# A two-stage attention and SwiGLU kernel: weight loads split by matrix, and a new order of work at the start of the first tile

## The chip, the cores and the metric

The kernel runs on one core of one Trainium2 chip. The metric is the device time of one execution in microseconds (us). Before the change three runs gave a median of 244.1 us (243.9 to 244.66). One more execution was recorded by the hardware profiler, and all times inside the kernel are from that one, counted from the start of its span.

The engines are called as the profile calls them: PE is TensorE (matrix products), DVE VectorE, ACT ScalarE, POOL GpSimd, SP SyncE. They run their own instruction lists in order and wait for each other by semaphores. PSUM is the memory that PE writes; it has eight banks here, each 128 x 512 float32.

## What is computed

For 4 batches, 8 heads, 768 positions and a head size of 64, an attention with a narrow window, and a SwiGLU block on its result:

```python
scores = scale * np.matmul(q, k.transpose(0, 1, 3, 2))
keep = is_global | is_local          # 8 global keys, 96 local ones
scores = np.where(keep, scores + bias, -1e9)
a = softmax(scores)
x = np.matmul(a, v)                  # heads side by side: 3072 tokens x 512
g = x @ w_gate                       # 512 x 1536
silu = g * (1.0 / (1.0 + np.exp(-g)))
out = (silu * (x @ w_val)) @ w_out   # 1536 x 512
```

## The kernel before

All work is emitted by one Python function in an order written out by hand; each engine executes its own instructions in that order. Inputs are float32 in memory and are cast to float16 by the loading DMAs, which POOL issues (k, q, v, all weights). The loads of one queue go out one after another; each uses one of eight semaphores in turn, so a ninth load is issued only after the first has landed.

**Two stages in one stream.** Tokens are worked in eight tiles of 384 (`TB`): tile t is half of batch t // 2. Attention gives `xT`, four chunks of 128 x 384 for each tile (c = 0 to 3: two from each quad of heads). The FFN of a tile runs over f = 0 to 11, each f being 128 of the 1536 hidden columns: a *gate* (four matmuls, one for each c, into one PSUM bank), a *value* (four more into another bank), and later `out_part`s (three matmuls of 512 columns each) that multiply the hidden tile with `w_out`. Attention work of the next half is put between the f steps.

**Gate and value** (`products`, `gate_or_val`, lines 538 to 564). After a gate's four matmuls ACT makes `th` = tanh(g/2) from the bank (L558) and DVE makes `sl` = (th + 1) * g from `th` and the bank (L560). After the value DVE multiplies it with `sl` into `hT` (L564). A bank is free for the next user when its last reader is done: a gate's bank after `sl`, a value's after `hT`.

**Banks.** Four banks a0 to a3 are handed out in turn by `bank`, three banks x0 to x2 by `spare`, and o0 is used by name. The head of the run uses all of them by name for batch 0's first half.

**The start** (lines 602 to 682). POOL issues k and q of the first half of batch 0, v, then gate and value weights in columns of two f (`load_w(0, 2)`: four DMAs), k and q of the second half for heads 0 to 3, weights for f 2 and 3, k and q for heads 4 to 7, weights for f 4 to 7, the rest of v, weights for f 8 to 11, then w_out. Each `load_w` goes through 256 rows at a time (g = 0 holds chunks c 0 and 1, g = 1 chunks 2 and 3). Meanwhile the four head pairs of the first half are turned (`p_tr`: transposes on PE, copies by DVE and ACT) and scored (`p_bias`, `p_sc`: a matmul that writes the position bias, then the scores on top), ACT takes the exponentials (L361), PE the sums (`denominators`) and products with v (`numerators`), DVE scales these into `xT` (L497). The part of v that belongs to chunk 3 is a small tile of its own, `vCut`.

Then the first FFN tile begins. Its first gates and values (f 0 and 1, lines 677 to 682) are started chunk by chunk as the chunks of `xT` become ready: c 0 and 1 of both, then c 2, then c 3.

**The rest of tile 0** (lines 762 to 770 and 824 to 843). For each f: gate, value, and after some f a step of the second half of batch 0: `trh(h0, h1)` turns two pairs (24 transposes into o0 and one spare bank; for pairs 0 and 1 all eight copies run on ACT, L316 and L330, for pairs 2 and 3 most run on DVE), `sch(hp)` scores one pair (it takes a0 to a3: six bias matmuls L339, then ten score matmuls L350, then four exponentials on ACT), `va(0, g, 1)` makes a half of `xT`. The order is: f 0, f 1, trh(0, 1), f 2, sch(0), f 3, sch(1), trh(2, 3), f 4, f 5, sch(2), f 6, sch(3), f 7, va, f 8, va, f 9 to 11.

**Tile 1's first steps** (line 771). `n_out` says after which f an `out_part` of tile 0 is put: (1, 0) means after f 0 and f 2. The part after f 2 is the fourth of the first row block, which needs the last piece of w_out; after f 2 too, two pairs of batch 1 are turned.

Of the kernel before, what the change touches and what calls it, by code (L numbers as in the profile page):

```python
# [9 lines left out]
FP32 = mybir.dt.float32  # L10
# [27 lines left out]
def kernel(  # L38
# [12 lines left out]
    nc = tc.nc  # L51
# [10 lines left out]
    NC = DM // 128  # L62
    J = S // 128
    NCH = 7
    TB = 384
# [25 lines left out]
    sb2 = ctx.enter_context(tc.tile_pool(name="sb2", bufs=2))  # L91
# [25 lines left out]
    def load_half(half, h0, h1):  # L117
        for st, src in ((k16, k), (q16, q)):
            nc.gpsimd.dma_start(out=st[:, half, h0:h1], in_=half_of(src, half, h0, h1))  # L119
# [21 lines left out]
    def make_slope(eng, h):  # L141
        eng(slopeI[:, h, :], ident, -slopes[h] / scale)
# [63 lines left out]
    wg = sb.tile([128, NC, DFF], FP16, name="wg")  # L206
    wv = sb.tile([128, NC, DFF], FP16, name="wv")
    wo = sb.tile([128, NFF, DM], FP16, name="wo")
    def load_w(f0, f1):
        a, z = 128 * f0, 128 * f1  # L210
        for g in range(2):
            for w, src in ((wg, moe_w_gate), (wv, moe_w_val)):
                nc.gpsimd.dma_start(  # L213
                    out=w[:, 2 * g:2 * g + 2, a:z],
                    in_=src[256 * g:256 * g + 256, a:z].rearrange("(p s) f -> p s f", s=2))

    def load_wo(g):
        nc.gpsimd.dma_start(
            out=wo[:, 3 * g:3 * g + 3, :],
            in_=moe_w_out[384 * g:384 * g + 384].rearrange("(f p) d -> p f d", p=128))  # L220
# [4 lines left out]
    def x_of(t):  # L225
        if t not in xTs:
            xTs[t] = sb2.tile([128, NC, TB], FP16, name="xT", tag="xT", bufs=4)
        return xTs[t]
# [5 lines left out]
    def bank(name, dt=FP32):  # L234
        tag = state["tags"][state["n"] % len(state["tags"])]
        state["n"] += 1
        return single(name, tag, dt)

    def banks(name, dt=FP32):
        return [bank(name, dt) for _ in range(2)]  # L240

    def spare(name, dt=FP32):
        tag = state["x"][gv.get("n", 0) % len(state["x"])]
        gv["n"] = gv.get("n", 0) + 1
        return single(name, tag, dt)

    def single(name, tag, dt=FP32):
        return ps.tile([128, 512 if dt == FP32 else 1024], dt, name=name, tag=tag)
# [8 lines left out]
    def run_later(n):  # L257
        for _ in range(n):
            if later:
                later.pop(0)()  # L260
# [273 lines left out]
    hTs = {}  # L534

    gv = {}

    def products(t, f, which, c0, c1, dst=None):
        if f == 0 and which == 0 and c0 == 0:
            hTs[t] = sb2.tile([128, NFF, TB], FP16, name="hT", tag="hT", bufs=3)  # L540
        if c0 == 0:
            if dst is None:
                dst = spare("gv"[which] + "ps")
            gv[f, which] = dst
        w = (wg, wv)[which]
        for c in range(c0, c1):
            nc.tensor.matmul(  # L547
                gv[f, which][:, 0:TB], lhsT=w[:, c, 128 * f:128 * f + 128],
                rhs=x_of(t)[:, c, :],
                start=(c == 0), stop=(c == NC - 1))  # L550

    def gate_or_val(t, f, which, c0=0):
        products(t, f, which, c0, NC)
        dst = gv.pop((f, which))

        if which == 0:
            th = sb2.tile([128, TB], FP32, name="th", tag="th")
            nc.scalar.activation(out=th, in_=dst[:, 0:TB], func=AF.Tanh, scale=0.5)  # L558
            sl = sb2.tile([128, TB], FP32, name="sl", tag="sl")
            nc.vector.scalar_tensor_tensor(  # L560
                out=sl, in0=th, scalar=1.0, in1=dst[:, 0:TB], op0=AluOp.add, op1=AluOp.mult)
            gv["sl"] = sl
        else:
            nc.vector.tensor_mul(hTs[t][:, f, :], dst[:, 0:TB], gv["sl"])  # L564

    ops_t = {}

# [34 lines left out]
    for c in range(3):  # L602
        load_v_rest(0, c)
    nc.gpsimd.dma_start(
        out=vCut[NG:NG + cut], in_=v[0, :, 3 * KC:TB, :].rearrange("h p d -> p h d"))
# [9 lines left out]
    def p_bias(hp, which, *tags):  # L615
        pairs[0, hp].sc = pairs[0, hp].bias(0, which, [single("sc", t) for t in tags])

    def p_sc(hp, which, *tags):
        if tags:
            p_bias(hp, which, *tags)  # L620
        pairs[0, hp].scores_half(0, which, pairs[0, hp].sc)

    def p_tr(hp, kt, qt, q_eng):
        tr = [single("trs", t, FP16)[:, 0:TB] for t in (qt, kt)]
        pairs[0, hp].turn_half(0, tr)
        pairs[0, hp].copy_half(0, tr, V, q_eng)

    V, A = nc.vector.tensor_copy, nc.scalar.copy
# [8 lines left out]
    nc.sync.dma_start(out=vCut[0:NG], in_=vG[:, 0])  # L637
    for h in range(4, 8):
        make_slope(nc.vector.tensor_scalar_mul, h)
    load_w(0, 2)  # L640
    load_half(1, 0, 4)
    load_w(2, 4)
    load_half(1, 4, 8)
    load_w(4, 8)
    for c in range(3, NCH):
        load_v_rest(0, c)
    load_w(8, 12)
    load_wo(0)
    load_wo(1)
    load_wo(2)  # L650
# [5 lines left out]
    for c in range(NCH):  # L656
        load_v_rest(1, c)
    p_bias(0, 0, "a0", "a1")
    p_tr(1, "x2", "o0", V)
    p_sc(0, 0)  # L660
    p_sc(0, 1, "a2", "a3")
    p_sc(1, 0, "x0", "x1")
    p_tr(2, "a0", "a1", V)
    p_sc(1, 1, "x2", "o0")
# [9 lines left out]
    for side, tag in enumerate(("x0", "x1")):  # L674
        quads[0, 1].numerators(side, single("num", tag))

    head = [(0, 0), (0, 1), (1, 0), (1, 1)]
    hb = [banks("gvps"), banks("gvps")]
    for c0, c1, f0, f1 in ((0, 2, 0, 2), (2, 3, 0, 1), (3, 4, 0, 1), (2, 4, 1, 2)):
        for f, which in head:  # L680
            if f0 <= f < f1:
                products(0, f, which, c0, c1, hb[f][which])

    def sc(b, *units):
        def step():
# [14 lines left out]
    def va(b, g, half):  # L702
        return lambda: quads[b, g].values(half, bank, nc.vector)
# [7 lines left out]
    def trh(h0, h1, by_engine):  # L711
        def step():
            b0, b1 = single("trs", "o0", FP16), spare("trs", FP16)
            (a, b), (c, d) = [(t[:, 0:TB], t[:, TB:2 * TB]) for t in (b0, b1)]
            k_eng, last = (V, V) if by_engine else (A, A)
            pair_of = [(h0, (c, a)), (h1, (d, b))] if by_engine else [(h0, (b, a)), (h1, (d, c))]
            for hp, tr in pair_of:
                pairs[0, hp].turn_half(1, tr)
            for hp, tr in pair_of:
                pairs[0, hp].copy_half(1, tr, k_eng, A if hp == h0 else last)  # L720
        return step

    def sch(hp):
        def step():
            p = pairs[0, hp]
            scs = [p.bias(1, 0), p.bias(1, 1)]
            for which in range(2):
                p.scores_half(1, which, scs[which], which == 1 and hp != 1)
        return step
# [9 lines left out]
    def first(t, b):  # L739
        return {(t, 2): [tr(b, 0), tr(b, 1)],  # L740
                (t, 4): [sc(b, (0, 0), (0, 1), (1, 0))],
                (t, 5): [tr(b, 2), tr(b, 3)],
                (t, 6): [sc(b, (1, 1), (2, 0), (2, 1))],
                (t, 8): [sc(b, (3, 0), (3, 1))],
                (t, 9): [va(b, 0, 0)],
                (t, 10, 1): [va(b, 1, 0), lambda: run_later(len(later))]}
# [11 lines left out]
    def second(t, b):  # L758
        return {(t, 0): [sc(b, (0, 2), (1, 2))], (t, 3): [sc(b, (2, 2), (3, 2))],
                (t, 7): [vas(b, 1)]}  # L760

    half1 = {(0, 1): [trh(0, 1, False)], (0, 2): [sch(0)],
             (0, 3): [sch(1), trh(2, 3, True)], (0, 5): [sch(2)], (0, 6): [sch(3)],
             (0, 7): [va(0, 0, 1)], (0, 8): [va(0, 1, 1)]}

    def ff(t, f0, f1, n_out=(0,)):
        return [(t, f, n_out[(f - f0) % len(n_out)]) for f in range(f0, f1)]

    stretches = [
        (ff(0, 0, 10) + ff(0, 10, 12, (1,)), half1),  # L770
        (ff(1, 0, 4, (1, 0)) + ff(1, 4, 10, (1,)) + ff(1, 10, 12, (2,)), first(1, 1)),
        (ff(2, 0, 12, (1,)) + ff(3, 0, 12, (1,)), both(2, 1)),
        (ff(4, 0, 12, (1,)) + ff(5, 0, 12, (1,)), both(4, 2)),
        (ff(6, 0, 12, (1,)), second(6, 3)),
# [2 lines left out]
    loads, after = {}, {}  # L777
# [41 lines left out]
    def take(step_list):  # L819
        run_later(len(later))  # L820
        for step in step_list:
            step()

    for tiles, steps in stretches:
        for t, f, n_out in tiles:
            for ld in loads.pop((t, f), []):
                ld()
            if f == 0:
                while any(fn.__name__ in ("spread", "spread_first", "scale") for fn in later):
                    run_later(1)  # L830
            for which in range(2):
                run_later(1)
                gate_or_val(t, f, which, NC if t == 0 and f < 2 else 0)
                for fn in after.pop((t, f, which), []):
                    fn()
            for n in range(n_out):
                if (t, f, n) in steps:
                    take(steps.pop((t, f, n)))
                run_later(1)
                out_part(*outs.pop(0))  # L840
            if (t, f) in steps:
                take(steps.pop((t, f)))
        assert not steps
# [40 lines left out]
```

## Time and profile before

| | us |
|---|---|
| runs, median | 244.1 |
| runs, lowest and highest | 243.9, 244.66 |
| profiled execution, whole | 244.26 |
| its span, first to last instruction | 242.5 |
| PE busy | 235.2 (97% of the span) |
| DVE, ACT, POOL busy | 166.1, 129.2, 96.7 |
| PE idle, 15.60 to 28.18 | 12.58 - 11.27 = 1.31 |
| PE idle, 28.18 to 47.60 | 0.00 |
| PE idle, 47.60 to 60.00 | 0.52 |
| PE idle, 60 to 231 | 0.00 |

How to read it. PE's busy time is the union of its matmuls, and a matmul of 384 columns is shown with 0.33 us though the next one starts 0.16 us after it: they overlap. So a gate's four matmuls take 0.65 us of PE's time (the gates from 37.86 and 39.17 us have their values at 38.52 and 39.82), and a wait shorter than about 0.16 us beyond the usual step does not appear as idle time at all. What PE loses is best read from starts: when did this matmul start, and when would it have, had it followed the one before at the usual step? The granted TensorE clock is full in all 40 slices of the span. HBM reads and writes come to 144 GB/s over the span, but the first 50 us move near 200 GB/s of landed data, and there the DMAs are always busy.

### The profile page before, as it was taken

To read this page: it belongs to the slowest core of one execution; us is meant where nothing else is said; L and a number is where in the kernel's file an instruction comes from. 1 tells how busy PE (TensorE), PEld (TensorE's weight loads), DVE (VectorE), ACT (ScalarE), POOL (GpSimd) and SP (SyncE) were. 2 spreads that over 40 slices of the span, in tenths; PEclk is the share of its full clock that TensorE was granted. 3 is DMA by queue.
4 is the path that set the end of the run, shared out by engine and by line. 5 is a ranking of instruction groups with operands and counts; after the bars stand their busy time and mean duration, and the time that the engine had idled before them with its cause. 6 is when DMAs were issued, how large, how long until landed. Compare 5 with 4: busy or idle time off the path is not lost.

```text
span 242.5 us, 6053 instructions
## 1 busy us (share of the span) xinstructions
PE 235.2 (97%) x2428; PEld 135.4 (56%) x2428; DVE 166.1 (68%) x355; ACT 129.2 (53%) x294; POOL 96.7 (40%) x117
## 2 busy tenths in 40 slices
PE   7999899999999999999999999999999999999994
PEld 4555466565565556555565556555565556555543
DVE  5675749878797768767796658767786558655530
ACT  5738476787864664374454574375355535233311
POOL 8989573665990000997053242900030223000000
PEclk9999999999999999999999999999999999999999
DMA  7999999999999736799219939970110110111022
GB/s 144 162 188 193 180 206 205 195 188 138 135 136 97 167 79 123 82 116 156 54 46 95 146 83 154 99 83 1 43 46 3 43 43 3 46 43 45 0 89 87
DMA packets 84612, 25.10 MB, mean 104 GB/s; under 512 B 72816, under 2 KB 81640, under 8 KB 84584
## 3 DMA queue, kind: packets, MB, share of 16 engines
q0 software_dynamic: 65296, 14.05, 65.8%
q1 hardware_dynamic: 18856, 10.39, 17.4%
q8 instruction: 19, 0.31, 0.5%
q10 hardware_dynamic: 432, 0.27, 0.4%
q14 instruction: 9, 0.07, 0.1%
HBM read 28.67 MB, written 6.29 MB: 144 GB/s over the span
## 4 chain that ended last, share of the span: by engine, by line
PE 78%; DMA 14%; POOL 5%; ACT 1%; issue 1%; POOLq 0%
PE ops L576 24%; PE gps L547 23%; PE vps L547 22%; DMA wv<-in_moe_w_val_dram 7%; DMA wo<-in_moe_w_out_dram 5%; PE sc L379 3%; PE num L439 3%; DMA vS<-in_v_dram 3%; PE den L439 2%; PE trs L273 1%; POOL wg L213 1%; PE ops L592 1%; POOL k L119 1%; POOL q L119 1%; POOL wv L213 1%; POOL vS L171 1%
## 5 line engine op out<-in xcount | busy, mean ns | idle before, releaser
L560 DVE SCALAR_TENSOR_TENSOR sl<-th,gps 128x384 f32<-128x384 f32 x94 | 51.9, 552 | 39.8 <-ACT th L558 39.0
L558 ACT ACTIVATE th<-gps 128x384 f32<-128x384 f32 x94 | 46.6, 496 | 59.5 <-PE gps L547 54.4
L547 PE MATMUL gps<-xT,wg 128*128 128x384 f16 x376 | 76.9, 327 | 0.5 <-DMA wg<-in_moe_w_gate_dram 0.5
L547 PE MATMUL vps<-xT,wv 128*128 128x384 f16 x376 | 76.8, 326 | 0.5 <-DMA wv<-in_moe_w_val_dram 0.4
L576 PE MATMUL ops<-wo,hT 128*128 128x512 f16 x276 | 73.3, 379 | 0.4 <-DMA wo<-in_moe_w_out_dram 0.4
L564 DVE TENSOR_TENSOR hT<-vps,sl 128x384 f16<-128x384 f32 x94 | 52.1, 554 | 8.6 <-PE gps L547 0.5
L547 PEld LDWEIGHTS <-wg 128*128 128x128 f16 x384 | 35.1, 98 | 31.6 <-issue 1.6
L547 PEld LDWEIGHTS <-wv 128*128 128x128 f16 x384 | 37.3, 98 | 27.0 <-DMA wv<-in_moe_w_val_dram 1.3
L576 PEld LDWEIGHTS <-hT 128*128 128x128 f16 x276 | 26.9, 98 | 24.1 <-issue 0.6
L387 ACT ACTIVATE at<-sc 128x432 f16<-128x432 f32 x72 | 33.9, 532 | 10.8 <-PE sc L379 10.8
L516 POOL TENSOR_TENSOR xT<-ns,rb 128x384 f16<-128x384 f32 x10 | 9.8, 994 | 66.7 <-ACT ns L512 35.4
L171 POOL DMA_DIRECT2D vS<-in_v_dram x28 | 24.7, 898 | 4.3 <-DMA kst<-in_k_dram 1.7
L582 ACT ACTIVATE osb<-ops 128x512 f32<-128x512 f32 x23 | 13.7, 598 | 14.4 <-PE ops L576 14.3
L398 POOL TENSOR_TENSOR at<-at,masks 128x864 f16<-128x864 f16 x4 | 7.3, 1822 | 23.9 <-ACT at L387 19.3
L398 DVE TENSOR_TENSOR at<-at,masks 128x864 f16<-128x864 f16 x20 | 12.2, 609 | 5.3 <-ACT at L387 5.3
L194 POOL DMA_DIRECT2D kst<-in_k_dram x16 | 14.0, 895 | 2.3 <-PE gps L547 1.2
L194 POOL DMA_DIRECT2D qst<-in_q_dram x16 | 13.8, 889 | 1.8 <-DMA vS<-in_v_dram 0.9
L361 ACT ACTIVATE at<-sc 128x432 f16<-128x432 f32 (+2 forms) x32 | 11.6, 445 | 5.2 <-PE sc L350 5.0
L512 ACT COPY ns<-num 128x384 f32<-128x384 f32 x20 | 8.1, 493 | 9.3 <-PE num L439 9.3
L439 PE MATMUL num<-at,vS 128*32 128x216 f16 (+6 forms) x560 | 11.2, 226 | 0.0
L395 DVE TENSOR_TENSOR at<-at,masks 128x432 f16<-128x432 f16 x24 | 8.1, 377 | 4.0 <-ACT at L387 4.0
L449 DVE STREAM_TRANSPOSE dT<-den 128x384 f32<-128x384 f32 x16 | 9.3, 581 | 1.7 <-PE den L439 1.1
(74 smaller groups left out, 179.6 us busy)
## 6 DMA issues: line engine op xcount, KB each, us to landing
out_dram<-osb SPq DMA_DIRECT2D x23, 256.0 KB
vS<-in_v_dram POOLq DMA_DIRECT2D x24, 120.0 KB, 5.6
wo<-in_moe_w_out_dram POOLq DMA_DIRECT2D x4, 384.0 KB, 10.2
qst<-in_q_dram POOLq DMA_DIRECT2D x16, 96.0 KB, 4.9
kst<-in_k_dram POOLq DMA_DIRECT2D x16, 90.0 KB, 4.9
wg<-in_moe_w_gate_dram POOLq DMA_DIRECT2D x4, 256.0 KB, 7.7
wv<-in_moe_w_val_dram POOLq DMA_DIRECT2D x4, 256.0 KB, 7.7
kst<-in_k_dram POOLq DMA_DIRECT2D x2, 384.0 KB, 12.0
```

The source lines that it names most:

```text
L171: nc.gpsimd.dma_start(out=vSs[b][NG:NG + n, c, :, :], in_=v[b, :, KC * c:KC * c + n, :].rearrange("h p d -> p h d"))
L194: nc.gpsimd.dma_start(out=st[b][p0:p0 + n, h // 2, :, h % 2, :], in_=src[b, h, 0:n * J].rearrange("(t p) d -> p t d", p=n))
L361: nc.scalar.activation(out=at[:, hi, 0:col + n], in_=sc[hi][:, 0:col + n], func=AF.Exp, scale=scale)
L387: nc.scalar.activation(out=at[:, hi, :], in_=sc[hi][:, 0:BANK], func=AF.Exp, scale=scale)
L398: mul_eng.tensor_mul(at, at, m[:, :, o:o + BANK])
L439: nc.tensor.matmul(dst[r, o:o + n], lhsT=ones[:, 0:32] if side is None else vals[:, 4 * g + j, side::2], rhs=pairs[b, 2 * g + j // 2].at[c ...
L547: nc.tensor.matmul(gv[f, which][:, 0:TB], lhsT=w[:, c, 128 * f:128 * f + 128], rhs=x_of(t)[:, c, :], start=(c == 0), stop=(c == NC - 1))
L558: nc.scalar.activation(out=th, in_=dst[:, 0:TB], func=AF.Tanh, scale=0.5)
L560: nc.vector.scalar_tensor_tensor(out=sl, in0=th, scalar=1.0, in1=dst[:, 0:TB], op0=AluOp.add, op1=AluOp.mult)
L564: nc.vector.tensor_mul(hTs[t][:, f, :], dst[:, 0:TB], gv["sl"])
L576: nc.tensor.matmul(ops, lhsT=hTs[t][:, f, 128 * i:128 * i + 128], rhs=wo[:, f, :], start=(f == 0), stop=(f == NFF - 1))
L582: nc.scalar.mul(out=osb, in_=ops, mul=0.5)
```

## The change

Three things are changed, and one order of out parts.

- `load_w` takes one matrix and four f at a time (512 columns: rows of 2 KB read, 1 KB written) instead of both matrices and two or four f. Gate weights for f 0 to 3 come in place of both matrices' weights for f 0 and 1; the value weights for f 0 to 3 come behind k and q of heads 0 to 3, in place of both matrices' weights for f 2 and 3. For f 4 to 7 and 8 to 11 all gate weights come before all value weights. There are 12 weight DMAs of 256 KB (as landed) in place of 8 of 128 KB and 8 of 256 KB.
- Tile 0 starts with the gates of f 0 to 3 in a0 to a3, chunk by chunk, and no value. The list `tile0` then gives the order of the rest up to f 8; values follow between the steps. `sl` of the first four f lies in the four buffers of `ns`, so that four can wait for their values.
- In the head of the run pair 0's scores come before pair 1's transposes.
- The second out part of tile 1 is put after f 3 instead of f 2.

```diff
-    def load_w(f0, f1):
-        a, z = 128 * f0, 128 * f1
+    def load_w(w, f0):
+        a, z = 128 * f0, 128 * f0 + 512
+        src = moe_w_gate if w is wg else moe_w_val
         for g in range(2):
-            for w, src in ((wg, moe_w_gate), (wv, moe_w_val)):
-                nc.gpsimd.dma_start(
-                    out=w[:, 2 * g:2 * g + 2, a:z],
-                    in_=src[256 * g:256 * g + 256, a:z].rearrange("(p s) f -> p s f", s=2))
+            nc.gpsimd.dma_start(
+                out=w[:, 2 * g:2 * g + 2, a:z],
+                in_=src[256 * g:256 * g + 256, a:z].rearrange("(p s) f -> p s f", s=2))
...
-            sl = sb2.tile([128, TB], FP32, name="sl", tag="sl")
+            if t == 0 and f < 4:
+                sl = sb2.tile([128, TB], FP32, name="sl", tag="ns", bufs=4)
+            else:
+                sl = sb2.tile([128, TB], FP32, name="sl", tag="sl")
...
-            gv["sl"] = sl
+            gv["sl", f] = sl
         else:
-            nc.vector.tensor_mul(hTs[t][:, f, :], dst[:, 0:TB], gv["sl"])
+            nc.vector.tensor_mul(hTs[t][:, f, :], dst[:, 0:TB], gv.pop(("sl", f)))
...
-    load_w(0, 2)
+    load_w(wg, 0)
     load_half(1, 0, 4)
-    load_w(2, 4)
+    load_w(wv, 0)
     load_half(1, 4, 8)
-    load_w(4, 8)
+    load_w(wg, 4)
+    load_w(wv, 4)
     for c in range(3, NCH):
         load_v_rest(0, c)
-    load_w(8, 12)
+    load_w(wg, 8)
+    load_w(wv, 8)
...
     p_bias(0, 0, "a0", "a1")
-    p_tr(1, "x2", "o0", V)
     p_sc(0, 0)
     p_sc(0, 1, "a2", "a3")
+    p_tr(1, "x2", "o0", V)
     p_sc(1, 0, "x0", "x1")
...
-    head = [(0, 0), (0, 1), (1, 0), (1, 1)]
-    hb = [banks("gvps"), banks("gvps")]
-    for c0, c1, f0, f1 in ((0, 2, 0, 2), (2, 3, 0, 1), (3, 4, 0, 1), (2, 4, 1, 2)):
-        for f, which in head:
-            if f0 <= f < f1:
-                products(0, f, which, c0, c1, hb[f][which])
+    hb = [bank("gps") for _ in range(4)]
+    for c0, c1 in ((0, 2), (2, 3), (3, 4)):
+        for f in range(4):
+            products(0, f, 0, c0, c1, hb[f])
...
-    half1 = {(0, 1): [trh(0, 1, False)], (0, 2): [sch(0)],
-             (0, 3): [sch(1), trh(2, 3, True)], (0, 5): [sch(2)], (0, 6): [sch(3)],
-             (0, 7): [va(0, 0, 1)], (0, 8): [va(0, 1, 1)]}
+    tile0 = [(0, 0), (1, 0), trh(0, 1, False), (2, 0), (3, 0), (0, 1), (1, 1), sch(0),
+             (2, 1), (3, 1), sch(1), trh(2, 3, True), (4, 0), (5, 0), sch(2), (4, 1), (5, 1),
+             (6, 0), (6, 1), sch(3), (7, 0), (7, 1), va(0, 0, 1), (8, 0), (8, 1), va(0, 1, 1)]
...
-        (ff(0, 0, 10) + ff(0, 10, 12, (1,)), half1),
-        (ff(1, 0, 4, (1, 0)) + ff(1, 4, 10, (1,)) + ff(1, 10, 12, (2,)), first(1, 1)),
+        (ff(0, 9, 10) + ff(0, 10, 12, (1,)), {}),
+        (ff(1, 0, 4, (1, 0, 0, 1)) + ff(1, 4, 10, (1,)) + ff(1, 10, 12, (2,)), first(1, 1)),
...
+    for item in tile0:
+        if callable(item):
+            take([item])
+            continue
+        f, which = item
+        run_later(1)
+        gate_or_val(0, f, which, NC if f < 4 and which == 0 else 0)
+        for fn in after.pop((0, f, which), []):
+            fn()
```

In `tile0` a pair (f, 0) is a gate and (f, 1) a value. For f 0 to 3 the gate's matmuls have been issued before, so that (f, 0) issues only `th` and `sl` there.

More of the change, by code (lines that the diff above doesn't have):

```diff
@@ L832 @@
                 run_later(1)
-                gate_or_val(t, f, which, NC if t == 0 and f < 2 else 0)
+                gate_or_val(t, f, which)
                 for fn in after.pop((t, f, which), []):
```

## The prediction

> **What bounds the kernel now.** I read the page's slices first, then the windows, then PE's timeline.
>
> ```profile
> PE   7999899999999999999999999999999999999994
> ...
> PEclk9999999999999999999999999999999999999999
> DMA  7999999999999736799219939970110110111022
> ```
>
> PE is full in every slice but the first two, one near 27 us and the last, at full clock. The windows say the same: PE is idle 0.00 us from 28.18 to 47.60 and 0.00 from 60 to 231. Work that is only moved can gain nothing there. All that can be won lies in the places where PE waits before 60 us. The wait view names few engines for them, so I took PE's timeline and looked at starts:
>
> ```profile
> 16.62 0.49 PE L547 MATMUL gvps<-xT,wv 128*128 128x384 f16 x2
> 17.39 0.32 PE L547 MATMUL gvps<-xT,wg 128*128 128x384 f16 x1 [0.28 <-DVE xT L497]
> ...
> 20.37 1.08 PE L547 MATMUL vps<-xT,wv 128*128 128x384 f16 x4
> 21.29 0.76 PE L339 MATMUL sc<-dist,slopeI 128*128 128x72 f16 x6
> ...
> 25.59 0.50 PE L547 MATMUL gps<-xT,wg 128*128 128x384 f16 x2
> 26.58 0.50 PE L547 MATMUL gps<-xT,wg 128*128 128x384 f16 x2 [0.49 <-DMA wg<-in_moe_w_gate_dram]
> 26.91 0.49 PE L547 MATMUL vps<-xT,wv 128*128 128x384 f16 x2
> 27.84 0.50 PE L547 MATMUL vps<-xT,wv 128*128 128x384 f16 x2 [0.45 <-DMA wv<-in_moe_w_val_dram]
> ...
> 46.99 0.81 PE L547 MATMUL vps<-xT,wv 128*128 128x384 f16 x4
> 48.20 0.81 PE L576 MATMUL ops<-wo,hT 128*128 128x512 f16 x3 [0.40 <-DMA wo<-in_moe_w_out_dram]
> ```
>
> The columns are start, length, engine, line, operation and count; in brackets what the wait ended with. Each matmul of 384 columns is followed 0.163 us later by the next (four: 0.65). So PE loses 17.39 - (16.62 + 0.33) = 0.44 for chunk 2 of xT; 0.14 more for chunk 3 (17.85 instead of 17.71); 21.29 - (20.37 + 0.65) = 0.27 for value weights of f 2 and 3; 26.58 - 25.92 = 0.66 and 27.84 - 27.24 = 0.60 for weights of f 4; 48.20 - 47.64 = 0.56 for w_out. Sum: **2.67 us**. These are the only prizes after 15.6 us.
>
> **The head of the run (pair 0's scores first).** PE now loses 0.45 at 6.16 and 0.42 at 6.94 waiting for pair 1's k and q. After the change pair 0's scores come there. They need DVE's copy L323, which ends at 5.69 + 0.59 = 6.28, so they start at 6.3, and pair 1's transposes at about 7.06 (scores 0.29, bias 0.27, scores 0.18) instead of 6.16. From those transposes to the end of DVE's qT copy is 6.16 to 7.90 less the 0.44 that q was late, some 1.6 with the copies at their usual pace: 8.67. So pair 1's scores start at 8.71, not 8.44. Then pair 2's transposes no longer wait for q (0.17 at 9.11), and a wait for bank a1 costs some 0.1: PE arrives at the numerators about 0.15 late. There it waits 0.24 today for vCut, a DMA issued before any that the change touches (13.40 in the timeline), so the delay is swallowed. I take 0; without that cover it costs 0.15, and at the best it gains nothing, since vCut lands when it does. Bounds: 0 to +0.3.
>
> **Four gates open.** The 16 matmuls stay 16. Eight run on chunks 0 and 1 from 15.63, then PE waits for chunk 2 as now (0.44 stays). At 17.39 there are now four on chunk 2 (to 18.04), then four on chunk 3, ready at 17.81. All end at 18.69, where before it was 18.82: the 0.14 goes. Their weights are 512 KB, as before; the last of that amount landed at 9.88 + 5.2 = 15.1.
>
> **A new wait.** Pairs 0 and 1 are turned from 18.78 (0.09 after the last gate's step, as now) to 19.57; then come values 0 and 1 (1.30) to 20.87. Then sch(0) writes a0 to a3. These hold the four gates, and a2 and a3 are free only after `sl` of f 2 and 3. But on ACT's queue `th` of f 2 and 3 stand behind the eight copies of trh(0, 1):
>
> ```profile
> 18.21 0.98 ACT L558 ACTIVATE th<-gvps 128x384 f32<-128x384 f32 x2 [3.34 <-PE gvps L547]
> 19.48 0.60 ACT L316 COPY kT<-trs 128x96 f16<-128x96 f16 x3 [0.29 <-PE trs L299]
> 19.96 0.51 ACT L330 COPY qT<-trs 128x384 f16<-128x384 f16 x1
> 20.33 0.65 ACT L316 COPY kT<-trs 128x96 f16<-128x96 f16 x3
> 20.80 0.56 ACT L330 COPY qT<-trs 128x384 f16<-128x384 f16 x1
> 21.18 0.58 ACT L558 ACTIVATE th<-gps 128x384 f32<-128x384 f32 x1
> ```
>
> The copies start 0.57 after the first transpose (19.48 - 18.92): at 19.35. The first `th` behind them starts 1.70 later: 21.04, ends 21.62. The second ends at 21.95 (ACT's step is 0.4 when it queues). DVE makes `sl` of f 2 from 21.65 to 22.21 and that of f 3 from 22.13 to 22.67 (0.56 each, step 0.47). PE has meanwhile done the bias matmuls into a0 and a1 (0.23, to 21.10). It writes a2 at 22.25 and a3 at 22.71. From a3's matmul to the next gate or value are 0.69 today (21.70 to 22.39): 23.40 instead of 22.39 for the same amount of work. **PE is 1.0 us later at this point, having waited 1.41.** Queued behind the waiting matmul are sch(0)'s scores and all later PE work; nothing else runs short from it.
>
> **What the delay covers.** Values 0 and 1 need 512 KB of value weights. In this slot of the queue they landed at 20.9 today (15.25 + 5.7). Rows of 1 KB written instead of 512 B land a little faster: in the trace 128 KB pieces landed 0.67 apart (17.84, 18.52, 19.19), 256 KB ones 1.28 apart (23.95, 25.23, 26.53, 27.80). That is 0.08 less for each of four pairs: 0.3 us for the first 1 MB, so 20.6 or sooner. PE can wait for them until 21.05 at no cost, because a2 is not free before. Issue time doesn't matter: four POOL issues of 0.71 fall away, but POOL itself waits for landings (0.73 before 13.14), so the DMAs are the slower part. Cover gone, each us past 21.05 is a us.
>
> The Trainium skill, "DMA: Bandwidth & Descriptors", Specifications, gives 512 B as the smallest transfer for line rate. Both row sizes reach that, so by it the wider rows gain 0 and the weights land at 20.9, still under the cover; the sum would be the same.
>
> **The rest of tile 0.** Value 2 from 23.40, value 3 from 24.05 (its bank x1 is free when hT of f 0 ends at 23.16), sch(1) 24.70, trh(2, 3) 25.80 (x2 free at 23.6), gates 4 and 5 from 26.59. Gate weights of f 4 to 7 are now the first two pieces behind k and q: they land near 24.9. So the 0.66 goes. Then sch(2) at 27.89, values 4 and 5 at 28.99, whose weights land near 27.5: the 0.60 goes. f 6, sch(3), and f 7 at 32.69, where it is 32.99 today. The banks in this stretch are free 0.3 us or more ahead by the same steps of ACT and DVE. Check: +1.41 - 0.14 - 0.27 - 0.66 - 0.60 = -0.26, the same within rounding.
>
> **w_out.** Its last piece landed at 48.2; the out part that needs it now follows f 3 and two transposes: PE is there near 50. The 0.56 goes. Late next is nothing: o0 is reused 1.3 us later, and ACT's copy out of it (0.60) falls into a gap between `th` steps. If ACT were late there, it would cost up to 0.6.
>
> **Sum.** -0.14 - 0.27 - 0.66 - 0.60 - 0.56 + 1.41 = **-0.82 us**. From 60 us on nothing changes. Profiled execution: 244.26 - 0.82 = 243.44 (span 241.7). It stood 0.16 over the median of the runs; from the median: 244.1 - 0.8 = **243.3**.
>
> **Rivals.**
> 1. *The gain is eaten.* The DMAs of the runs without a profiler may land sooner, so that part of the 2.1 us of DMA waits isn't there to be won, or ACT's queue is 0.3 later than I add up. For it: PE margin at 21.05 is slim, and the head has up to +0.3. Time: 244.1 - 0.3 = 243.8 (243.4 to 244.5). Against the first part: runs and profile differ by 0.16 only. It also covers a change that doesn't do what it says: rows of 2 KB that land no faster.
> 2. *Slower.* The value weights of f 0 to 3 are the last to land. One place, PE's first value matmul on chunk 2. It decides from a landing at 21.05 + 0.82 = 21.9; by 0.3% from 22.6. Instruction fetches of 16 KB go through the same DMAs, and the piece that landed at 20.9 today was 1.0 later than its neighbours' 0.67 step; one more such delay, plus the 0.3 that the wider rows should bring not coming, gives 21.9 to 22.9. Time: 244.1 to 245.1. Against it: the pieces land in order at an even pace all along.
> 3. *The banks don't bind.* If ACT makes the four `th` ahead of the copies, the 1.41 goes: 244.1 - 2.2 = 241.9. Against it: the written order of ACT's queue.
>
> **Chances.** Forecast 0.52, rival 1 0.34, rival 2 0.09, rival 3 0.05. The forecast's own spread is 242.8 to 243.7: steps read to 0.1, some eight of them, and three runs that lie 0.76 apart. About 0.3% (0.73 us) is what a measurement tells from no change: below 243.37 is faster, and my forecast stands right at it. Two thirds of the forecast, a quarter of rival 1 and all of rival 3 lie below: 0.49. Slower by over 0.3% are most of rival 2 and the far end of rival 1: 0.08. Range: 242.3 to 244.5, which leaves out rival 3's centre and the upper end of rival 2.
>
> **What would show it.** Right: PE's first bias matmul into the third bank starts near 22.2 and waits for DVE's `sl`; no wait for weights at gate 4 or value 4; no wait at w_out; PE at f 7 near 32.7. Wrong: a wait for `wv` at 20 to 22 that is longer than the bank wait; `th` of f 2 before ACT's copies; pair 1's copies so late that numerators start after 13.4; a new wait after 48 us at o0 or for exponentials.

## The result, and the profile after

Six runs of the changed kernel have a median of 243.53 us (243.44 to 243.65), six of the kernel before beside them 244.0 (243.51 to 244.66): ratio 0.998, 95% interval 0.9964 to 0.9996. That is 0.5 us, 0.2%, and so within the 0.3% that was set as the bound. The profiled execution took 243.63 instead of 244.26 (span 241.9 instead of 242.5).

The page of the changed kernel, busy tenths in 40 slices:

```profile
PE   7898999999999999999999999999999999999994
...
PEclk9999999999999999999999999999999999999999
DMA  8999999999992636899119939960110110111022
```

Each slice is 6 us. The low slice of before at 24 to 30 us, where the weights of f 4 were late, now reads 9; in its place the slices at 6 to 12 and at 18 to 24 us read 8. From 24 us on nothing is lost that the page can show. The windows of the changed kernel (start and end, length, PE busy, then PEld, DVE, ACT, POOL, clock, DMA share, GB/s):

```profile
15.60:28.18 12.58, 11.19 (x140) 6.80 (x131) 7.74 (x20) 7.30 (x22) 7.79 (x11) 1.00 1.53 191
28.18:47.60 19.42, 19.42 (x242) 11.59 (x240) 15.23 (x31) 13.21 (x34) 11.73 (x15) 1.00 1.30 202
47.60:60.00 12.40, 12.27 (x157) 7.63 (x158) 10.36 (x22) 10.43 (x25) 9.07 (x13) 1.00 2.13 170
```

PE's idle time from 15.60 to 28.18 is 12.58 - 11.19 = 1.39 us, hardly other than the 1.31 of before. From 47.60 to 60.00 it went from 0.52 to 0.13. So the first stretch, where five of the six waits lay, lost as much as it won. PE's timeline of the changed kernel says with what:

```profile
15.83 1.47 PE L547 MATMUL gps<-xT,wg 128*128 128x384 f16 x8
17.59 1.46 PE L547 MATMUL gps<-xT,wg 128*128 128x384 f16 x8 [0.28 <-DVE xT L497]
...
19.77 1.48 PE L547 MATMUL vps<-xT,wv 128*128 128x384 f16 x8
21.08 0.39 PE L339 MATMUL sc<-dist,slopeI 128*128 128x72 f16 x4
22.46 0.81 PE L339 MATMUL sc<-dist,slopeI 128*128 128x432 f16 x2 [0.98 <-DVE sl L563]
23.20 0.48 PE L350 MATMUL sc<-qT,kT 64*128 64x72 f16 x10
23.61 1.47 PE L547 MATMUL vps<-xT,wv 128*128 128x384 f16 x8
...
26.81 1.47 PE L547 MATMUL gps<-xT,wg 128*128 128x384 f16 x8
```

The gates follow one another with one wait, for chunk 2 of `xT` (0.44 by starts). The values of f 0 and 1 start at 19.77 without a wait. Then comes the new one: the bias matmul into the third bank stands until 22.46 for DVE's `sl` of f 2. From the first bias matmul of pair 0 to the next value are 23.61 - 21.08 = 2.53 us. In the kernel before the same work took 1.10, from 21.29 to the gate in its timeline's line

```profile
22.39 0.82 PE L547 MATMUL gps<-xT,wg 128*128 128x384 f16 x4
```

So **1.43 is lost**. Gates 4 and 5 follow at 26.81 without a wait for weights.

ACT's queue in the changed kernel:

```profile
18.59 0.87 ACT L558 ACTIVATE th<-gps 128x384 f32<-128x384 f32 x2 [3.53 <-PE gps L547]
19.54 0.60 ACT L316 COPY kT<-trs 128x96 f16<-128x96 f16 x3
20.02 0.51 ACT L330 COPY qT<-trs 128x384 f16<-128x384 f16 x1
20.39 0.65 ACT L316 COPY kT<-trs 128x96 f16<-128x96 f16 x3
20.86 0.56 ACT L330 COPY qT<-trs 128x384 f16<-128x384 f16 x1
21.23 0.97 ACT L558 ACTIVATE th<-gps 128x384 f32<-128x384 f32 x2
```

The gates of f 2 and 3 were complete on PE by 19.05, but their `th` starts only at 21.23, behind eight copies.

The end of tile 0's weights is gone as a place to wait; PE's timeline of the changed kernel at w_out:

```profile
46.93 0.81 PE L547 MATMUL vps<-xT,wv 128*128 128x384 f16 x4
47.67 0.53 PE L273 MATMUL trs<-ident,kst 128*64 128x128 f16 x12
```

After that value PE goes straight on with transposes, and the out part comes at 50.44, when the last piece of w_out (47.33) has long been there.

### The profile page after: what moved, and what is told of

Read it like the earlier page. It is cut to its first block, busy times and chain, and to the rows that moved or that the text cites. A ratio compares the mean times of both kernels' runs of the same rounds, so it can differ in the third digit from the quotient of the medians.

```text
span 241.9 us, 6047 instructions
## 1 busy us (share of the span) xinstructions
PE 235.0 (97%) x2428; PEld 136.1 (56%) x2428; DVE 165.3 (68%) x355; ACT 129.2 (53%) x294; POOL 93.9 (39%) x113
## 4 chain that ended last, share of the span: by engine, by line
PE 92%; ACT 2%; DVE 2%; DMA 2%; issue 0%; SPq 0%; DVEq 0%
PE gps L547 26%; PE vps L547 25%; PE ops L579 24%; PE num L439 4%; PE sc L379 3%; PE den L439 2%; PE sc L339 2%; DMA q<-in_q_dram 2%; PE sc L350 2%; PE trs L273 1%; PE ops L595 1%; PE trs L299 1%; DVE sl L563 1%; ACT th L558 1%; ACT kT L316 0%; ACT at L387 0%
## 5 line engine op out<-in xcount | busy, mean ns | idle before, releaser
L558 ACT ACTIVATE th<-gps 128x384 f32<-128x384 f32 x96 | 47.4, 497 | 61.9 <-PE gps L547 56.7
L563 DVE SCALAR_TENSOR_TENSOR sl<-th,gps 128x384 f32<-128x384 f32 x96 | 52.8, 552 | 39.9 <-ACT th L558 39.2
L547 PE MATMUL gps<-xT,wg 128*128 128x384 f16 x384 | 77.9, 327 | 0.3 <-DVE xT L497 0.3
L547 PE MATMUL vps<-xT,wv 128*128 128x384 f16 x384 | 77.6, 326 | 0.0
L567 DVE TENSOR_TENSOR hT<-vps,sl 128x384 f16<-128x384 f32 x96 | 53.1, 554 | 9.2 <-PE vps L547 1.3
```

The source lines that it names most:

```text
L547: nc.tensor.matmul(gv[f, which][:, 0:TB], lhsT=w[:, c, 128 * f:128 * f + 128], rhs=x_of(t)[:, c, :], start=(c == 0), stop=(c == NC - 1))
L563: nc.vector.scalar_tensor_tensor(out=sl, in0=th, scalar=1.0, in1=dst[:, 0:TB], op0=AluOp.add, op1=AluOp.mult)
L567: nc.vector.tensor_mul(hTs[t][:, f, :], dst[:, 0:TB], gv.pop(("sl", f)))
```

## The experiments

All were timed beside the kernel before on the same chip. Its median was 243.69, 243.84 and 243.94 in the three groups of runs (243.0 to 246.65 over 93 runs), so ratios are given.

### What makes PE wait for the third bank

The changed kernel, with the four `th` and `sl` ahead of the two pairs' transposes and copies:

```diff
-    tile0 = [(0, 0), (1, 0), trh(0, 1, False), (2, 0), (3, 0), (0, 1), (1, 1), sch(0),
+    tile0 = [(0, 0), (1, 0), (2, 0), (3, 0), trh(0, 1, False), (0, 1), (1, 1), sch(0),
```

> The changed kernel with one edit: th and sl of f 2 and 3 are put ahead of the turning of pairs 0 and 1 on ACT. Theory (the banks a2 and a3 hold PE for 1.36 us because their tanh stands behind eight copies): the wait of 0.98 + 0.12 us of idle time at 22.46 and 22.92 goes, PE reaches f 7 at 31.6 instead of 32.92, the time falls by 1.2 to 1.4 us against the changed kernel: 242.2 us, 0.9925 of before. Rival (the bank wait only covers DMA waits that come back once it is gone): PE waits for wv at the first values or at f 4 and 5 instead, by about 1 us, and the time stays within 0.4 us of the changed kernel: 243.2 us.

Measured: 242.66 (242.19 to 243.0), ratio to before 0.9946 (0.9926 to 0.9966). PE's timeline of this kernel:

```profile
19.61 1.47 PE L547 MATMUL vps<-xT,wv 128*128 128x384 f16 x8
20.93 0.76 PE L339 MATMUL sc<-dist,slopeI 128*128 128x72 f16 x6
...
22.39 1.46 PE L547 MATMUL vps<-xT,wv 128*128 128x384 f16 x8 [0.30 <-ACT qT L330]
...
34.79 0.49 PE L547 MATMUL vps<-xT,wv 128*128 128x384 f16 x2
35.69 0.50 PE L547 MATMUL vps<-xT,wv 128*128 128x384 f16 x2 [0.41 <-DMA wv<-in_moe_w_val_dram]
```

The bank wait is gone: six bias matmuls in one go from 20.93. The edit moves nothing on PE, and on DVE nothing stands between the two places, so the cause is shown: the order of ACT's queue. But not all of 1.43 arrives at the end. Value 2 waits 0.36 for a spare bank that ACT's copies now free later (22.39 instead of 22.03). And PE, now earlier, meets the value weights of f 8, which landed at 35.65: 35.69 instead of 35.12, 0.57. The head was 0.15 earlier here (first gate 15.68). 1.43 - 0.36 - 0.57 + 0.15 = 0.65, against 0.66 between the spans (241.86 and 241.20). PE was at f 7 at 31.70, where 31.6 was expected; the expected fall of 1.2 to 1.4 us came to about 0.8 by the ratios. The two waits that came back are those of one execution: with the old head put in as well (below) they were 0.20 and 0.14.

An attempt to cover the wait at f 8 on top of that, with the last `va` between its gate and its value:

```diff
-             (6, 0), (6, 1), sch(3), (7, 0), (7, 1), va(0, 0, 1), (8, 0), (8, 1), va(0, 1, 1)]
+             (6, 0), (6, 1), sch(3), (7, 0), (7, 1), va(0, 0, 1), (8, 0), va(0, 1, 1), (8, 1)]
```

> The changed kernel with th and sl of f 2 and 3 ahead of the turning, and in addition the value of f 8 behind the second va. Theory (once the bank wait is gone PE comes early enough to wait 0.57 us for the last value weights, landed at 35.65): that wait goes, since the value now starts near 36.0, and the time falls by 0.5 us against the kernel with the first edit alone: 242.1 us. Rival (the next wait takes it over, for w_out's last piece or for tile 1's xT): within 0.2 us of that kernel: 242.6 us.

Measured: 243.18 (242.71 to 245.24), ratio 0.9973 (0.9951 to 0.9995). A gain was expected; by the ratios it is 0.3% worse than without it, though the intervals overlap. PE's timeline of this kernel, in its slowest execution (245.24):

```profile
39.24 0.81 PE L547 MATMUL vps<-xT,wv 128*128 128x384 f16 x4
40.74 0.81 PE L547 MATMUL gps<-xT,wg 128*128 128x384 f16 x4 [0.69 <-DVE hT L567]
```

The wait moved to DVE: the multiply that frees the value bank of f 8 now stands behind the second `va`'s work there, and PE loses 0.85. Whether the edit also takes away the wait at f 8 can't be read here: PE was 1.9 us late in this execution, and the value weights (36.11) would have been there in any case.

### Whether the wider rows mattered

The changed kernel with the first four f of both matrices loaded in eight DMAs of 256 columns:

```diff
...
+        n = 256 if f0 == 0 else 512
         for g in range(2):
-            nc.gpsimd.dma_start(
-                out=w[:, 2 * g:2 * g + 2, a:z],
...
+            for a in range(128 * f0, 128 * f0 + 512, n):
+                nc.gpsimd.dma_start(
+                    out=w[:, 2 * g:2 * g + 2, a:a + n],
...
```

> The changed kernel with the first four f of both matrices loaded in eight DMAs of 256 columns (rows of 1 KB read) instead of four of 512 columns. Theory of the prediction (wide rows bring the weights 0.3 us sooner, which the bank wait covers): value weights of f 0 to 3 land 0.2 to 0.4 us later than 19.4, at 19.6 to 19.8, PE's waits stay those of the changed kernel, and the time is that of the changed kernel within 0.1 us: 243.4 us. Rival (rows of 2 KB are what makes the change faster): weights land 1 us later, PE waits for them at the first values, and the time rises by 0.5 us or more.

Measured: 243.38 (243.18 to 243.85), ratio 0.9977 (0.9958 to 0.9996), the changed kernel's own. The value weights landed at 17.97, 19.02, 19.71 and 20.46, with the wide rows at 18.10 and 19.38. The last is 1.08 later, where 0.2 to 0.4 was expected; but the last piece holds f 2 and 3, and those that values 0 and 1 need were complete at 19.71. PE's timeline of this kernel:

```profile
19.97 1.47 PE L548 MATMUL vps<-xT,wv 128*128 128x384 f16 x8
21.28 0.39 PE L340 MATMUL sc<-dist,slopeI 128*128 128x72 f16 x4
22.66 0.81 PE L340 MATMUL sc<-dist,slopeI 128*128 128x432 f16 x2 [0.99 <-DVE sl L564]
```

PE's values start 0.20 later than with wide rows, as much as its numerators do (13.55 against 13.35), so not for the weights; and the bank wait is the same. With wide rows the last of these weights landed at 19.38 to 20.00 in eight executions, so the narrow rows are 0.5 to 1.1 later in the one execution there is, in a place where nobody waits for it. That the bank wait covers a late landing is seen in the kernel of the next section, whose out part is put back: its value weights landed at 20.00 and PE's values took 0.07 longer for them, yet it wrote the third bank at 22.34, against 22.33 in a second execution of the changed kernel, whose values started at the same time (19.65 and 19.64) and did not wait. A landing after 21.05, where the cover should end, is in none of the traces of this load order.

### The out part

Moved back in the changed kernel:

```diff
-        (ff(1, 0, 4, (1, 0, 0, 1)) + ff(1, 4, 10, (1,)) + ff(1, 10, 12, (2,)), first(1, 1)),
+        (ff(1, 0, 4, (1, 0)) + ff(1, 4, 10, (1,)) + ff(1, 10, 12, (2,)), first(1, 1)),
```

And the reverse edit of the same line, alone, in the kernel before, so that the part moves there too.

> The changed kernel with the out part put back after f 2 of tile 1. Theory of the prediction (the later out part takes away the wait for the last piece of w_out, 0.56 us in the kernel before): the piece lands at 47.3 now and PE arrives at 47.6, so a wait of 0 to 0.2 us comes back: 243.5 to 243.7 us. Rival (the out part's new place is what saved the 0.56 us): the time rises by 0.5 us to 244.0 us.

> The kernel before with the out part alone moved after f 3 of tile 1. Theory (the wait of 0.56 us for w_out is on the path and nothing is late behind it): the time falls by 0.5 to 0.6 us, to 243.45 us, 0.9977 of before, which is all that the whole change brought. Rival (o0 or ACT is late next and takes it back): within 0.15 us of before.

Measured: moved back, 243.4 (243.21 to 243.79), ratio 0.9982 (0.9964 to 0.9999). Moved alone, 243.46 (243.05 to 244.46), ratio 0.9982 (0.9962 to 1.0003). PE's timelines, of the changed kernel with the part moved back:

```profile
46.82 0.81 PE L547 MATMUL vps<-xT,wv 128*128 128x384 f16 x4
47.70 0.81 PE L579 MATMUL ops<-wo,hT 128*128 128x512 f16 x3
```

and of the kernel before with the part moved:

```profile
46.52 0.81 PE L547 MATMUL vps<-xT,wv 128*128 128x384 f16 x4
47.26 0.53 PE L273 MATMUL trs<-ident,kst 128*64 128x128 f16 x12
```

With the other parts in, w_out lands at 47.66 and the old place costs 47.70 - 47.47 = 0.23, which the runs don't show. In the kernel before it cost 0.56 in the profiled execution; in that of the kernel with the part moved alone the piece landed at 47.30, so there the old place would have cost some 0.17 (PE was ready at 47.17). The median of the move alone is as forecast, but its interval includes no change. And the parts don't add up: the move alone has the ratio 0.9982, the change without the move 0.9982, both together 0.9981. The intervals overlap too far to say which part the 0.2% comes from.

### The head of the run

Three kernels: the changed one with the old head, the first experiment's with the old head, and the kernel before with the new head alone.

For the first two:

```diff
+    p_tr(1, "x2", "o0", V)
     p_sc(0, 0)
     p_sc(0, 1, "a2", "a3")
-    p_tr(1, "x2", "o0", V)
```

and its reverse for the third.

> The changed kernel with pair 1's transposes put back ahead of pair 0's scores. Theory (the new order delays pair 1's scores by waiting for its copies, 0.66 us of idle time at 9.16, and nothing swallows it when vCut lands early): the first gate starts 0.2 to 0.4 us sooner than 15.83 and the time falls by 0.2 to 0.4 us: 243.2 us. Rival (the 0.20 us are due to the first load of q, which landed 0.8 us later in that execution; the order costs nothing): the first gate starts where it does with the same arrival of q, and the time stays within 0.1 us of the changed kernel: 243.5 us.

> The changed kernel with both edits: th and sl of f 2 and 3 ahead of the turning of pairs 0 and 1, and pair 1's transposes back ahead of pair 0's scores. Theory (the new head costs 0.4 to 0.6 us whenever vCut lands before 12.9, but keeps PE busy enough that its clock comes up by 7.2; the old head is sooner but leaves the clock low until about 10.4 in some executions): the lowest runs are 0.4 us or more under the lowest of the one-edit kernel (242.19), at 241.8 or less, single runs reach 244 or more, and the median is 242.2 to 242.7. Rival (the wide spread of the runs with the old head has nothing to do with the head): the spread stays within 0.9 us as with the new head.

> The kernel before with pair 0's scores moved ahead of pair 1's transposes, and nothing else. Theory of the prediction (the delay of pair 1's scores is swallowed by the wait for vCut): within 0.1 us of before. Theory now (vCut lands at 12.3 to 13.2 in most executions, so that nothing swallows it): the first gate starts at 15.7 to 15.9 in the profile, the lowest runs are 0.3 to 0.5 us above the lowest of before, the slowest runs of before (246) are absent, and the medians lie within 0.3 us.

Measured: changed with the old head 243.41 (242.76 to 245.81), ratio 0.9988 (0.9959 to 1.0017). The first experiment with the old head 242.45 (241.99 to 244.23), ratio 0.9947 (0.9928 to 0.9967). Before with the new head 243.72 (243.51 to 244.92), ratio 0.9993 (0.9979 to 1.0008). By medians no pair is told apart. The lowest runs are: the old head reaches 241.99 where the new one stops at 242.19; 242.76 where the changed kernel's own lowest is 242.85; and 243.0 (of many more runs) where the new head alone stops at 243.51. All three point the same way, by 0.1 to 0.5 us, but the numbers of runs and in part the chips differ, so this is a hint and no more. The traces were expected to show the first gate sooner than 15.83 with the old head in the changed kernel, and at 15.7 to 15.9 with the new head alone. It came at 16.58, in an execution whose clock rose only at 10.42, and at 15.39. The lowest run of the second kernel was expected at 241.8 or less and is 241.99.

What the new head does is seen in PE's timelines. The kernel before:

```profile
12.73 0.43 PE L439 MATMUL num<-at,vS 128*32 128x216 f16 x12
13.40 0.20 PE L439 MATMUL num<-at,vCut 128*32 128x24 f16 x4 [0.24 <-DMA vCut<-in_v_dram]
...
15.63 0.50 PE L547 MATMUL gvps<-xT,wg 128*128 128x384 f16 x2
```

The changed kernel:

```profile
5.56 0.53 PE L299 MATMUL trs<-ident,q 128*64 128x128 f16 x6 [0.31 <-ACT q L635]
6.03 0.81 PE L339 MATMUL sc<-dist,slopeI 128*128 128x432 f16 x2
6.76 0.36 PE L350 MATMUL sc<-qT,kT 64*128 64x216 f16 x4
...
7.50 0.36 PE L299 MATMUL trs<-ident,k 128*64 128x128 f16 x6
...
9.16 0.36 PE L350 MATMUL sc<-qT,kT 64*128 64x216 f16 x4 [0.66 <-DVE qT L330]
...
13.35 0.43 PE L439 MATMUL num<-at,vS 128*32 128x216 f16 x12
13.61 0.19 PE L439 MATMUL num<-at,vCut 128*32 128x24 f16 x4
```

The kernel before with the new head alone:

```profile
6.33 0.36 PE L350 MATMUL sc<-qT,kT 64*128 64x216 f16 x4 [0.33 <-DVE kT L323]
...
7.06 0.36 PE L299 MATMUL trs<-ident,k 128*64 128x128 f16 x6
...
8.72 0.36 PE L350 MATMUL sc<-qT,kT 64*128 64x216 f16 x4 [0.66 <-DVE qT L330]
...
12.91 0.43 PE L439 MATMUL num<-at,vS 128*32 128x216 f16 x12
```

With the new head pair 1's scores come so soon behind its transposes that PE waits 0.66 for their copies. With the old head pair 0's scores fill that time, and PE's waits lie ahead of the transposes, where k and q are late. From pair 0's scores to the numerators the two kernels with the new head take the same time: 6.59 in the changed kernel, 6.58 with the head alone, and 6.58 in the forecast (6.3 to 12.88). What differs is where this stretch starts. With the head alone it starts at 6.33, as forecast, and the numerators are 0.18 late. In the changed kernel it starts at 6.76, because in that execution pair 0's q came late (it is turned from 5.56, from 5.04 with the head alone, from 4.91 in the kernel before) and PE ran at half speed until 6.61. So of the 0.62 by which its numerators are later than before (13.35 and 12.73), 0.44 belong to the execution and 0.18 to the order. Whether the old head would have taken up a late q isn't shown: in its one execution with a q as late (5.53) the clock stayed low.

Behind the numerators the kernel before lost 13.40 - (12.73 + 0.26) = 0.41 to `vCut`; 0.26 is the step in the other two. That swallows 0.41 of the 0.62, and the first gate is 0.20 later. But this cover belongs to one execution as well: `vCut` landed at 13.36 there and at 12.09 to 13.15 in the twelve others. Without it the order costs more. In the kernel before with the out part moved, which has the old head, the numerators start at 12.58 and the first gate at 15.07; with the new head alone they start at 12.91 and 15.39, 0.32 to 0.33 later, with q turned at 5.00 and 5.04 and the clock up at 4.95 and 5.34. With a later rise of the clock the old head has 12.67 (rise at 6.43, the first experiment's kernel) and the new one 13.19 to 13.35 (6.61 to 7.16, four kernels). The remaining ones can't be compared: two have the extra matmuls of the next section (12.90 and 13.37), the narrow rows (13.55) waited for a late q of pair 2, and two had half the clock past 10 us. So the traces put the cost at 0.3 to 0.7 us, from single executions; the medians don't resolve it.

### Whether PE's early idle time spreads the runs

Some runs of kernels with the old head are 1 to 2 us above the others (and one run with the new head, the 245.24 above). One idea was that PE's idle time at 5 to 7 us delays the clock's rise, so I put matmuls without use there, in the kernel before and in the best one:

```diff
     p_bias(0, 0, "a0", "a1")
+    fill(4)
     p_tr(1, "x2", "o0", V)
```

> The kernel before with four more warm-up matmuls of 256 columns (0.43 us at full clock, 0.85 us at half) in PE's gap between the first bias matmuls and pair 1's transposes; their product is used by nothing. Theory (the old head leaves PE so idle between 5 and 8 us that the clock comes up a window later in some executions, and that is what makes its runs spread from 243.0 to 246): the runs above 244.3, nine of 35 before, become rare, and the lowest stay within 0.3 us of before's lowest. Rival (the spread comes from the first loads' landing times or from elsewhere): the spread and the share of runs above 244.3 stay.

> The changed kernel with th and sl of f 2 and 3 first, the old head, and the same four warm-up matmuls in the gap. Theory (as for the kernel before with the fill): the runs above 243.5, two of 12 without the fill, go, the lowest stay near 242.0, median 242.2 to 242.4. Rival (the fill costs its own time because PE is not idle there at half clock): all runs 0.3 us or more above those without it, median 242.7.

Measured: before with the matmuls 244.23 (243.56 to 245.31), ratio 1.0005 (0.9976 to 1.0034), with 5 of 12 runs above 244.3; the best with them 242.46 (242.24 to 242.85), ratio 0.9945 (0.9929 to 0.996). Of the runs of before, 5 and 7 of 35 in the first two groups (not the "nine of 35" of the expectation) and 4 of 23 in this one were above 244.3. So the share did not go down in the kernel before. In the best kernel none of 6 runs is above 243.5, where 2 of 12 were, which is too few to tell. Nor did the clock rise sooner: at 6.38 and 6.41 with the matmuls, at 4.72, 4.95, 6.43 and 10.42 in the four old-head executions without them. The runs give the idea no support. PE's timeline of before with the matmuls, an execution with late loads:

```profile
47.34 0.81 PE L547 MATMUL vps<-xT,wv 128*128 128x384 f16 x4
49.20 0.81 PE L576 MATMUL ops<-wo,hT 128*128 128x512 f16 x3 [1.04 <-DMA wo<-in_moe_w_out_dram]
```

Here w_out landed at 49.15 and PE lost 1.21 to it, and 1.0 more to gate weights of f 4. So late DMAs are a source of loss in this slow run. Whether they are the main source of the spread stays open.

### The changed kernel again

> The changed kernel as it is, beside the others on the same chip, for its own size and spread. Theory: median 243.4, lowest 243.2, within 0.1 us of the kernels with the out part put back and with narrow rows, and no run above 244. Rival (the row width or the out part's place was worth something after all): 0.2 us or more under those two, at 243.2 or less.

Measured: 243.38 (242.85 to 244.2), ratio 0.9981 (0.9966 to 0.9996): the median as expected and the first result again, with one run above 244.

## Why the prediction came out as it did

The median of 243.53 lies 0.2 above the predicted 243.3; against before that is -0.5 where -0.8 was forecast. Point by point:

- **Where the prizes lie: right.** Of the six waits, the 0.44 for chunk 2 stayed as forecast, and the 0.14, 0.27, 0.66, 0.60 and 0.56 are gone. The sizes are those of one execution: in three others with the old loads PE lost 0.69, 0.93 and 0 to weights of f 2 and 3 (0.27 here) and 0.92, 1.32 and 1.67 to those of f 4 (1.26 here). (One reading was wrong without effect: the second slice of PE isn't among those that are not full, it reads 9.)
- **The new wait: right**, in place, cause and size. 1.41 was forecast, 1.43 measured; the third bank at 22.25 forecast, 22.46 measured, which is the head's 0.20. ACT's queue order was the cause, as the first experiment shows.
- **The cover of the value weights: right, its size too small.** They landed by 19.38, forecast 20.6 or sooner. The wider rows were priced at 0.3 (the steps give 0.07 for each pair, not 0.08). The last weights of f 0 to 3 landed at 19.38 to 20.00 in eight executions with wide rows and at 20.24 to 21.10 in five without, about 1 us sooner. Even the narrow rows (20.46) cost nothing.
- **Weights for f 4 and after, and f 7: right.** No wait at gate 4 or value 4; f 7 at 32.92, forecast 32.69, again the head.
- **The head: wrong.** The step that failed is "PE arrives at the numerators about 0.15 late. There it waits 0.24 today for vCut, a DMA issued before any that the change touches (13.40 in the timeline), so the delay is swallowed. I take 0". The first gate came at 15.83 instead of 15.63, **+0.20**. The delay was 0.62 and not 0.15: the order gave 0.18, as the kernel with the head alone shows, and a late q with a late clock the rest, which the sum had at nothing. And the cover, read from starts like the other waits, was 0.41 and not 0.24. So two terms were off by 0.47 and 0.17 and partly cancel. With +0.20 in place of 0 the sum is -0.82 + 0.20 = -0.62; the profiled executions differ by 243.63 - 244.26 = -0.63.
- **Where it was luck.** That this step cost no more is an accident of the two profiled executions. Where `vCut` landed sooner, the new head was 0.3 to 0.7 behind the old one, above the 0.15 that the prediction names for lost cover; in the medians this isn't resolved.
- **w_out: gone as forecast, but its size is one execution's.** Of the 0.56, 0.23 came back when the part was put back with the rest of the change in. The last piece of w_out landed at 47.30 to 49.15 in four executions with the old loads, and the wait was 0.11 with the head alone and 1.21 with the extra matmuls.

In this pair of executions the gain that seems missing is thus accounted for. Four gates and the loads removed 0.14 + 0.27 + 0.66 + 0.60 = 1.67 us of waits, and the bank wait and the head added 1.43 + 0.20 = 1.63. What remains is the wait for w_out. The runs don't confirm that last split, since the change without the move is as fast as with it. Of rival 1 ("the gain is eaten") the head's part came true, within its 0.3. Rival 3's condition, `th` ahead of the copies, was met by the first experiment; its gain of 2.2 came to about 1.3 by the ratio. In its profile PE, now earlier, ran into 0.93 us of waits for a spare bank and for the weights of f 8.

The best kernel is that first experiment, with either head: 242.45 to 242.66, some 0.5% below before and 0.3% to 0.4% below the changed kernel.

## What to carry to other kernels

When several producers' banks are held at once, follow each bank to its last reader and read what stands ahead of that reader in its engine's own queue: here eight copies ahead of a tanh cost 1.43 us, nearly as much as the waits for gate and value weights that the rewrite removed (0.27 + 0.66 + 0.60 = 1.53). A wait removed moves PE up to the next late load or copy, so only part of it arrives (here 0.65 of 1.43 + 0.15, between two profiles), and the next one has to be priced as well. Don't take the landing of one profiled execution as a fixed size, neither as cover for a delay nor as a prize: read the same landing in a second execution first.

## What the runs showed of the hardware

**The rise of the clock differs from execution to execution, and the page's clock row doesn't show it.** The row says 9 from the first slice, but the first pair of 432-column bias matmuls took 0.54 us in the profile of before, 0.81 in that of after and 0.90 in others. The line of the changed kernel (6.03) stands above, where its head is shown. PE's timeline of the changed kernel with the old head, where the clock rose only at 10.42:

```profile
5.99 0.90 PE L339 MATMUL sc<-dist,slopeI 128*128 128x432 f16 x2
...
10.03 0.52 PE L299 MATMUL trs<-ident,k 128*64 128x128 f16 x6
10.35 0.37 PE L299 MATMUL trs<-ident,q 128*64 128x128 f16 x6
```

Six transposes of one shape take 0.52 from 10.03 and 0.37 from 10.35. In the 13 traces the first record of a full clock lies between 4.26 and 10.42 us; ahead of it the row shows 9 all the same.

**It can fall again.** The windows of the kernel with the last `va` ahead of value 8, in an execution whose first loads were late (columns as above, the clock third from the end):

```profile
7.00:11.00 4.00, 2.41 (x38) 1.28 (x36) 2.35 (x8) 1.63 (x5) 3.53 (x6) 1.00 2.01 163
11.10:14.50 3.40, 3.40 (x43) 1.62 (x40) 1.57 (x6) 2.08 (x6) 2.99 (x6) 0.50 1.37 197
```

PE was busy for 2.41 of 4.00 us, then had half the clock from 11.09 to 14.50, 3.41 us, though it was busy throughout. The Trainium skill, "TensorE: Matmul & The Clock Gate", Part 1, "What's actually happening", gives a free-running window of about 3.4 us after which the clock is set by how busy the last one was; the 3.41 agrees. How busy a window must be is not shown by any run here.

**A load often lands late behind an instruction fetch.** Each of the 13 traces has one packet of 16 KB that fetches instructions between 17.9 and 20.9 us; it takes 0.89 to 0.97 us. In the profile of before it comes at 18.51, and the value weights land at 20.91, about 1 us behind the step of their neighbours. In eight of the traces one of the next three loads lands 0.4 to 1.4 us behind the usual step (0.67 for 128 KB, 1.28 for 256 KB, 1.0 for k and q), in the other five by 0.3 or less. The link is argued from times; no run was made to test it.
